# More filler products before the first batch's waits, and the second transposing read moved between the query and key moves

## The chip, the cores and the metric

The kernel runs on one core of a Trainium2 chip. The metric is the device time of one execution in microseconds (us), the median of several runs; lower is better.

## The reference

Strided sparse attention followed by a bilinear feed-forward layer. Shapes: q, k and v are 8 batches x 8 heads x 576 positions x 64; w_a and w_b are 512 x 1536, w_out is 1536 x 512; all inputs and the output are float32.

```python
scores = scale * np.matmul(q, k.transpose(0, 1, 3, 2))        # scale = 1/8
rel = pos[:, None] - pos[None, :]
mask_local   = (rel >= 0) & (rel < 32)
mask_strided = (rel >= 0) & (pos[None, :] % 32 == pos[:, None] % 32)
masks = [mask_local if h < 4 else mask_strided for h in range(8)]
attn = softmax(np.where(masks, scores, -1e9))
x = np.matmul(attn, v).transpose(0, 2, 1, 3).reshape(4608, 512)
out = ((x @ w_a) * (x @ w_b)) @ w_out
```

## The kernel before

**Two halves, woven together.** The feed-forward half works on nine tiles of 512 tokens (`t` = 0 to 8). A tile has 16 slots: 12 slots `ffn_ab`, one for each block `f` of 128 of the 1536 features (eight 128x128 by 128x512 products on TensorE, PE, in line 619; a copy on ScalarE, line 636; the product a*b on VectorE, lines 639 and 641), and 4 slots of output products (`ffn_y`, line 771, in tiles 0 and 1; `ffn_ys`, line 707, in tiles 2 to 8; `y_tail`, line 736, in the last). The attention half works on eight batches `b` of 576 tokens. Its steps are sent out between the slots, from tables written by hand: `STEPS` for batches 1 and 2, `LATER` for batches 3 to 7, by slot number. `take(i)` runs the attention steps due at slot `i`, and after it the functions registered with `do(i, ...)` for that slot run. All engines keep the written order (`manual_schedule`), and so does SP, the engine that issues most of the transfers inside the chip: an instruction that waits on SP holds back everything written behind it.

**Batch 0** comes before slot 0 and has an order of its own, the string `ORDER`. A name such as `Tk0p` is a part of a step: `Tk`/`Tq` transposes keys or queries on PE, `S` are scores (`p` the products, `x` the exponential on ScalarE, `m` the mask on VectorE), `V` is the product with the values (`p`) and its scaling (`r` a reciprocal, `n` the multiplication in line 489), `X` the transpose of the attention's output into `xT`, the feed-forward's input, and `F` the first feature blocks of tile 0. `*n` stands for `spin(n)`: n filler products of 128x128 by 128x224 constants on PE (line 154), whose results nobody reads.

**Batches 2 to 7** get their transposed keys and queries through `step_D`: VectorE transposes in blocks (line 326 for the first four heads, `z` = 0, in two parts; line 331 for the other four, `z` = 1, in three), and when the last part of the query is done, SP moves the pieces into place: for the query pair c=0 four transfers into `qz_buf` (line 345), then for the key pair c=1 two into `kT_buf` (line 341), then for the query pair c=1 four more. For batches 4 to 7, `step_D` of the last query part with `z` = 0 is registered for slot 16(b-2)+9.

**Batches 3 to 7, the first four heads' output.** It is written as rows to a scratch area in DRAM (`rows_out`, steps `O0` and `O1` in `LATER`, SP, line 504) and read back transposed into `xT` (`rows_in`, steps `I0` and `I1`, SP, line 509). `I1` of batch b is in `LATER` at 9, which is slot 16(b-1)+9: the same slot in which `step_D` of batch b+1 sends its moves, and ahead of them, since `take(i)` comes first.

```python
    LATER = {-1: "S0", 0: "S1", 1: "V0", 2: "S2", 3: "V1 O0", 4: "S3", 5: "V2", 6: "S4 I0", 7: "V3 O1", 8: "S5", 9: "V4 I1",
             10: "S6",
             11: "V5"}
```

The scores of the next batch begin one slot before the next tile (`-1: "S0"`, line 385) and read the pair c=0. The next tile's products read `xT` from its first slot on.

Of the kernel before, what the change touches and what calls it, by code (L numbers as in the profile page):

```python
# [14 lines left out]
FIRST_D = 2  # L15
# [15 lines left out]
def kernel(  # L31
# [11 lines left out]
    B, H, S, D = q.shape  # L43
# [134 lines left out]
    def blocks(nm, z):  # L178
        z = int(z)
        return sb.tile([128, 2, (S, RS * GP)[z]], BF16, tag=f"t{nm}{z}", name=f"t{nm}{z}", bufs=1)  # L180
# [138 lines left out]
    def step_D(b, z, nm, part):  # L319
        src = nats[b, nm, z == 1]  # L320
        if part == 0:
            tl[b, z, nm] = blocks(nm, z)
        t = tl[b, z, nm]
        if z == 0:
            i = slice(NY // 2 * part, NY // 2 * (part + 1))
            nc.vector.transpose(t.rearrange("p h (i y) -> p i h y", i=NY)[:, i],
                                src[:, i].rearrange("p i (h d) -> p i h d", h=2))
            last = part == 1
        else:

            nc.vector.transpose(
                t.rearrange("p h (r c) -> p r h c", r=RS)[:, :, :, YS * part:YS * part + 32],
                src[:, part].rearrange("p (r h d) -> p r h d", r=RS, h=2))
            last = part == 2
        if last:
            for nm, c in {"k": (("k", 0),), "q": (("q", 0), ("k", 1), ("q", 1))}[nm]:
                t = tl[b, z, nm]
                for e in range(2):
                    if nm == "k":
                        dst = kT_buf[b % 2][z][64 * e:64 * e + 64, c]  # L340
                        nc.sync.dma_start(out=dst[:, PAD:] if z == 0 else dst[:, :RS * GP], in_=t[64 * c:64 * c + 64, e])
                        continue
                    for j in range(2):
                        r0 = 64 * c + 32 * j
                        nc.sync.dma_start(out=qz_buf[b % 2][j][z][64 * e + 32 * j:64 * e + 32 * j + 32, c],
                                          in_=t[r0:r0 + 32, e])

    def rezero(b):

        for j in range(2):  # L350
            for t in qz_buf[b % 2][j]:
                nc.gpsimd.memset(t[32:64] if j == 0 else t[64:96], 0.0)
# [154 lines left out]
    def rows_in(b, c):  # L507

        nc.sync.dma_start(out=xT[:, c, S * (b % XR):S * (b % XR + 1)], in_=scratch.pop((b, c)), transpose=True)
# [51 lines left out]
    def step_X(b, c):  # L561
# [6 lines left out]
            "Xp": lambda c: X_p(0, c), "Xe": lambda c: X_e(0, c)}  # L568

    ORDER = """  # L570
        G0 C0 Tk0p *2 Tq0p Tk0e Tq0e *5 Tk1p S1p M G1 Tq1p S1x Tk1e *4 Tq1e S0p S1m *7 G2 C1 S0x S3p Tk2p Tq2p Tk2e S3x Tq2e *3
        S2p S2x V1p S0m *2 V1r S3m V0p V0r V1n V0n *2 S4p Tk3p Tk3e S2m Tq3p S4x Tq3e *2 S5p S5x X0p X0e *3 V2p V2r V3p V2n
        V3r V3n S6p V4p V4r V4n S6x X1p V5p V5r S7p X1e V5n V6p S7x F0A V6r V7p V6n X2p X2e Z F1A F0B V7r V7n F1B X3p F0b X3e
        F1b F0c F1c""".split()


# [2 lines left out]
                 12.6: "S1", 12.75: "L0 X2", 13: "s2 X3 V0 m2 L1 W3", 13.5: "V1 S3", 14: "V2 X0", 14.5: "V3 D1", 15: "X1"},  # L579
             2: {20: "S0", 20.5: "S1", 21.5: "V0", 22: "S2", 23: "V1", 23.5: "S3", 24.5: "V2", 25: "S4", 26: "V3", 26.5: "S5",  # L580
                 27.5: "V4", 28: "S6", 28.5: "V5", 29: "S7", 29.5: "V6", 30.5: "V7"}}
    LATER = {-1: "S0", 0: "S1", 1: "V0", 2: "S2", 3: "V1 O0", 4: "S3", 5: "V2", 6: "S4 I0", 7: "V3 O1", 8: "S5", 9: "V4 I1",
             10: "S6",
             11: "V5"}
    IN_Y = {2: "S7", 6: "V6", 11: "V7"}
    FN = {"Tk": step_Tk, "Tq": step_Tq, "S": step_S, "V": step_V, "X": step_X, "W": lambda b, n: fast_w(n, slice(0, 3)),
          "s": S_px, "m": S_m, "L": lead_vl, "O": rows_out, "I": rows_in, "Pk": lambda b, c: pair_up("k", c), "Pq": lambda b, c: pair_up("q", c),
          "Z": lambda b, n: zero_qz(0, nc.vector, ((1, 1),)), "D": lambda b, n: step_D(FIRST_D, 0, "k", n)}

    def run(b, slot):  # L590
# [4 lines left out]
    steps = {}  # L595
# [204 lines left out]
    with tc.manual_schedule(engines={ENG.PE, ENG.SP, ENG.Pool, ENG.DVE, ENG.Activation}):  # L800
# [76 lines left out]
        for b in range(1, B):  # L877
            for pos, names in (STEPS.get(b) or {16 * (b - 1) + x: n for x, n in LATER.items()}).items():
                steps.setdefault(pos, []).append((b, names.split()))
            if b not in STEPS:  # L880
                for n, names in IN_Y.items():
                    steps["y", b - 1, n] = [(b, names.split())]

        at = {}

# [12 lines left out]
        for b in range(FIRST_D, B):  # L898
            g0 = 16 * (b - 2)
            if b == FIRST_D:  # L900
                do(0, load_qk, b, False)
                do(1, load_qk, b, True)
                do(16, load_vl, b)
                for h in range(HL):
                    do(20 + h, load_vs, b, (h,))
            else:
                for h in range(HL):
                    do(g0 + h + (2 if b == FIRST_D + 1 else -2), load_qk, b, False, (h,))
                    do(g0 + h + (6 if b == FIRST_D + 1 else 2), load_qk, b, True, (h,))
                    do(g0 + h + 10, load_vs, b, (h,))  # L910
                do(g0 + (10 if b == FIRST_D + 1 else 7), load_vl, b)
            gs = {2: (14, 14, 15, 15, 16, 16, 17, 17, 18, 18), 3: (8, 9, 10, 11, 12, 13, 14, 15, 16, 17)}.get(b) or (
                3, 5, 7, 9, 12, 13, 14, 15, 16, 17)
            for (z, nm, part), g in zip(((0, "k", 0), (0, "k", 1), (0, "q", 0), (0, "q", 1), (1, "k", 0), (1, "k", 1),
                                         (1, "k", 2), (1, "q", 0), (1, "q", 1), (1, "q", 2)), gs):
                if (b, z, nm, part) != (FIRST_D, 0, "k", 1):
                    do(g0 + g, step_D, b, z, nm, part)
# [60 lines left out]
```

## Time and profile before

| | us |
|---|---|
| time, median of 3 runs (lowest, highest) | 328.95 (328.48, 330.82) |
| the profiled execution: its time | 331.59 |
| its span, first to last instruction | 329.6 |
| PE busy | 320.2 (97%) |
| VectorE (DVE) busy | 247.9 (75%) |
| ScalarE (ACT) busy | 183.5 (56%) |
| GpSimd (POOL) busy | 149.7 (45%) |
| mean granted TensorE clock | 0.987 of full |

The profile is of one execution. An engine's busy time is the sum over its instructions; those of PE overlap each other, so that a group of 12 products may show 1.47 us from its first start to its last end while the next group starts 1.31 us after it. The page cuts the span into 40 slices of 8.24 us and gives the busy share and the granted clock of PE for each, in tenths. In the timeline a row has the start in us, the duration in us, engine, line, operation, output and input, the count, and in brackets the idle time before it with what ended it. Rows of SPq are SP's queue issuing transfers: their duration is that of the issue, not of the landing.

### The profile page before, as it was taken

What the parts mean: (1) busy time and instruction counts of PE and PEld (TensorE: products, weight loads), DVE (VectorE), ACT (ScalarE), POOL (GpSimd) and SP (SyncE); (2) the same over time, 40 slices, a digit from 0 to 9 for tenths busy, and PEclk for the clock granted to TensorE, in tenths of its full rate; (3) what the DMA queues carried; (4) which work ended last, traced back from release to release, by engine and by line L of the source; (5) the groups of instructions that cost most, each with busy time, mean ns of one, the idle gap of its engine ahead of it and who ended that gap; (6) DMA issues with size and microseconds to landing.
All of it is one profiled execution on the core that took longest, in us unless ns stands there. A gap on an engine that the chain in (4) does not pass through costs nothing.

```text
span 329.6 us, 7240 instructions
## 1 busy us (share of the span) xinstructions
PE 320.2 (97%) x2597; PEld 204.6 (62%) x2624; DVE 247.9 (75%) x530; ACT 183.5 (56%) x305; POOL 149.7 (45%) x279
## 2 busy tenths in 40 slices
PE   7899999999999999999999999999999999999994
PEld 6664555455555578556999885559555954584474
DVE  7647687888868988898889888988977745726652
ACT  6744767358774476547654765467546643323341
POOL 8845836769857635762576337634101001100000
PEclk9959999999999999999999999999999999999998
DMA  9999999499999897999899999999145040004004
GB/s 156 153 204 194 204 183 165 136 161 144 119 234 118 152 109 76 113 206 137 93 126 182 173 100 100 173 185 113 45 107 139 16 127 0 3 0 129 0 0 127
DMA packets 110722, 40.41 MB, mean 123 GB/s; under 512 B 88672, under 2 KB 107744, under 8 KB 110688
## 3 DMA queue, kind: packets, MB, share of 16 engines
q0 software_dynamic: 85968, 19.48, 65.0%
q1 hardware_dynamic: 24576, 20.42, 24.6%
q8 instruction: 20, 0.33, 0.5%
q14 instruction: 14, 0.11, 0.1%
q10 hardware_dynamic: 144, 0.07, 0.1%
HBM read 39.51 MB, written 10.91 MB: 153 GB/s over the span
## 4 chain that ended last, share of the span: by engine, by line
PE 91%; DMA 3%; POOL 2%; DVE 1%; issue 1%; ACT 0%; POOLq 0%
PE mm L619 54%; PE mm L707 16%; PE mm L771 6%; PE st L385 4%; PE o L463 2%; PE o L522 2%; DMA vl<-in_v_dram 2%; PE mm L736 2%; PE ab L619 2%; POOL shared L196 1%; PE end L736 1%; DMA kT0l<-tk 1%; PE tp L547 1%; POOL vl L224 0%; PE tp L286 0%
## 5 line engine op out<-in xcount | busy, mean ns | idle before, releaser
L619 PE MATMUL mm<-xT,wb_sb 128*128 128x512 bf16 (+1 forms) x468 | 109.9, 357 | 0.5
L619 PE MATMUL mm<-xT,wa_sb 128*128 128x512 bf16 (+1 forms) x453 | 108.3, 356 | 0.7
L636 ACT COPY a_sb<-mm 128x512 f32<-128x512 f32 x106 | 62.0, 585 | 71.6 <-PE mm L619 70.7
L639 DVE TENSOR_TENSOR pf<-a_sb,mm 128x512 bf16<-128x512 f32 x84 | 57.3, 682 | 26.9 <-PE mm L619 22.4
L619 PEld LDWEIGHTS <-wb_sb 128*128 128x128 bf16 x480 | 46.7, 98 | 44.6 <-issue 1.1
L944 POOL CAST pace<-pf 1x1 f32<-1x1 bf16 x87 | 23.8, 274 | 110.8 <-DVE pf L639 94.2
L619 PEld LDWEIGHTS <-wa_sb 128*128 128x128 bf16 x480 | 43.8, 98 | 31.4 <-issue 0.2
L406 ACT ACTIVATE p<-st 72x576 bf16<-72x576 f32 (+1 forms) x56 | 36.4, 650 | 14.7 <-PE st L385 14.5
L538 DVE TENSOR_TENSOR xT<-o,xr 64x288 bf16<-64x288 f32 x48 | 21.4, 445 | 15.3 <-ACT xr L532 15.0
L707 PEld LDWEIGHTS <-ps 128*128 128x128 bf16 x288 | 28.0, 98 | 3.1
L707 PE MATMUL mm<-wf,ps 128*128 128x256 bf16 x216 | 25.5, 273 | 0.0
L684 ACT COPY y_sb<-mm 128x512 f32<-128x512 f32 (+1 forms) x28 | 15.5, 555 | 17.9 <-PE mm L707 14.5
L531 ACT ACTIVATE xr<-o 64x576 f32<-64x576 f32 x28 | 18.1, 647 | 12.2 <-PE o L522 12.0
L771 PE MATMUL mm<-wo_sb,pf 128*128 128x512 bf16 x93 | 23.1, 379 | 0.2
L242 POOL DMA_DIRECT2D vs<-in_v_dram x24 | 19.6, 818 | 5.1 <-PE mm L707 2.4
L707 PEld LDWEIGHTS <-pf 128*128 128x128 bf16 x216 | 20.3, 98 | 2.6 <-issue 0.2
L532 ACT ACTIVATE xr<-xr 64x576 f32<-64x576 f32 x28 | 19.1, 683 | 0.9
L707 PE MATMUL mm<-wo_sb,pf 128*128 128x256 bf16 x144 | 18.5, 273 | 0.1
L211 POOL DMA_DIRECT2D ql<-in_q_dram x24 | 16.1, 669 | 4.9 <-DMA wo_sb<-in_moe_w_out_dram 3.6
L211 POOL DMA_DIRECT2D kl<-in_k_dram x24 | 16.0, 668 | 4.9 <-issue 3.2
L641 DVE TENSOR_TENSOR pf<-a_sb,mm 128x512 bf16<-128x512 f32 x22 | 14.9, 676 | 4.3 <-ACT a_sb L636 2.7
L653 DVE TENSOR_TENSOR ps<-pf 128x512 bf16<-128x512 bf16 (+1 forms) x48 | 17.7, 380 | 0.4
(147 smaller groups left out, 453.3 us busy)
## 6 DMA issues: line engine op xcount, KB each, us to landing
out_dram<-y_sb SPq DMA_DIRECT2D x12, 512.0 KB, 4.9
out_dram<-y_sb SPq DMA_DIRECT2D x11, 256.0 KB, 3.0
vl<-in_v_dram POOLq DMA_DIRECT2D x6, 384.0 KB, 8.0
kl<-in_k_dram POOLq DMA_DIRECT2D x24, 72.0 KB, 3.2
ql<-in_q_dram POOLq DMA_DIRECT2D x24, 72.0 KB, 3.5
vs<-in_v_dram POOLq DMA_DIRECT2D x24, 72.0 KB, 4.2
wo_sb<-in_moe_w_out_dram POOLq DMA_DIRECT2D x4, 384.0 KB, 9.2
natk<-in_k_dram POOLq DMA_DIRECT2D x20, 72.0 KB, 3.6
```

The lines of the kernel that those rows point to most:

```text
L211: nc.gpsimd.dma_start(out=t[32 * h:32 * h + 32], in_=src[b, h].rearrange("(i y) d -> y i d", y=32))
L242: nc.gpsimd.dma_start(out=vs_buf[b % 2][:, h, :, 0:D], in_=v[b, HL + h].rearrange("(p r) d -> p r d", r=RS))
L406: nc.scalar.activation(p_flat(p)[:M, :2 * W].rearrange("p (i n) -> p i n", n=2 * n), st[:M].rearrange("p a (i n) -> p (a i) n", n=256)[:, ...
L531: nc.scalar.activation(r, sums, ACT.Ln)
L532: nc.scalar.activation(r, r, ACT.Exp, scale=-1.0)
L538: nc.vector.tensor_mul(dst.rearrange("d (p r) -> d p r", r=RS)[:, :, G * half:G * (half + 1)], o[:64, j, :W].rearrange("d (g p) -> d p g", ...
L619: nc.tensor.matmul(ps_[:, c0:c0 + n], lhsT=w[:, kk, 128 * f:128 * (f + 1)], rhs=xT[:, kk, x0:x0 + n], start=(kk == first and c0 == 0), sto ...
L636: nc.scalar.copy(a_sb, ab[0])
L639: nc.vector.tensor_mul(pf[:, f, :].rearrange("p (i a s) -> p a i s", i=2, s=16), halves(a_sb), halves(ab[1]))
L707: nc.tensor.matmul(bank[b][:, q], lhsT=lhs(g, q), rhs=rhs(g), start=k in "172" and q == 0 and g == 0, stop=g == FG - 1, skip_group_check=True)
L771: nc.tensor.matmul(ybank[j], lhsT=pf[:, f, 128 * j:128 * (j + 1)], rhs=wo_sb[:, f], start=(f == 0), stop=(f == FD - 1))
L944: nc.gpsimd.tensor_copy(pace, done)
```

## The change

There are two edits. In `ORDER`, three places get more fillers: after `Tk0p` 4 instead of 2, after `X0e` (before `V2p`) 5 instead of 3, and between `S6p` and `V4p` 4 where there were none. And `I1` is taken out of `LATER`; `step_D` now calls `rows_in(b - 1, 1)` itself, after the four moves of the query pair c=0 and before the moves of the key pair c=1, for b = 4 to 7, which are the reads of batches 3 to 6. For the last batch, which has no `step_D` after it, `I1` is appended to its old slot.

```diff
@@ step_D
                         nc.sync.dma_start(out=qz_buf[b % 2][j][z][64 * e + 32 * j:64 * e + 32 * j + 32, c],
                                           in_=t[r0:r0 + 32, e])
+                if (nm, c, z) == ("q", 0, 0) and b - 1 > FIRST_D:
+                    rows_in(b - 1, 1)
@@ ORDER
-        G0 C0 Tk0p *2 Tq0p Tk0e Tq0e *5 Tk1p S1p M G1 Tq1p S1x Tk1e *4 Tq1e S0p S1m *7 G2 C1 S0x S3p Tk2p Tq2p Tk2e S3x Tq2e *3
-        S2p S2x V1p S0m *2 V1r S3m V0p V0r V1n V0n *2 S4p Tk3p Tk3e S2m Tq3p S4x Tq3e *2 S5p S5x X0p X0e *3 V2p V2r V3p V2n
-        V3r V3n S6p V4p V4r V4n S6x X1p V5p V5r S7p X1e V5n V6p S7x F0A V6r V7p V6n X2p X2e Z F1A F0B V7r V7n F1B X3p F0b X3e
+        G0 C0 Tk0p *4 Tq0p Tk0e Tq0e *5 Tk1p S1p M G1 Tq1p S1x Tk1e *4 Tq1e S0p S1m *7 G2 C1 S0x S3p Tk2p Tq2p Tk2e S3x Tq2e *3
+        S2p S2x V1p S0m *2 V1r S3m V0p V0r V1n V0n *2 S4p Tk3p Tk3e S2m Tq3p S4x Tq3e *2 S5p S5x X0p X0e *5 V2p V2r V3p V2n
+        V3r V3n S6p *4 V4p V4r V4n S6x X1p V5p V5r S7p X1e V5n V6p S7x F0A V6r V7p V6n X2p X2e Z F1A F0B V7r V7n F1B X3p F0b X3e
@@ LATER
-    LATER = {-1: "S0", ..., 7: "V3 O1", 8: "S5", 9: "V4 I1",
+    LATER = {-1: "S0", ..., 7: "V3 O1", 8: "S5", 9: "V4",
@@ after the steps are entered
+        steps[16 * (B - 2) + 9][-1][1].append("I1")
```

## The prediction

> **What bounds the kernel now.** I read the page first, by engine and by slice, then the chain of waits, then what TensorE (PE) waited for, then the timelines of PE and of SP's queue around the places that the diff touches.
>
> ```profile
> PE 320.2 (97%) x2597; PEld 204.6 (62%) x2624; DVE 247.9 (75%) x530; ACT 183.5 (56%) x305; POOL 149.7 (45%) x279
> ...
> PE   7899999999999999999999999999999999999994
> ...
> PEclk9959999999999999999999999999999999999998
> ...
> PE 91%; DMA 3%; POOL 2%; DVE 1%; issue 1%; ACT 0%; POOLq 0%
> ```
>
> PE is busy 97% of the span and is 91% of the chain that ended last. So a change can give back only what PE loses to waits, or to a low clock. The clock row shows one hole: the third slice stands at half. Cut finer, in windows of half the hole's length (6.8 us, from 17.2 to 24.0):
>
> ```profile
> 13.81:17.22 3.41, 2.44 (x61) 1.98 (x59) 1.88 (x6) 1.76 (x4) 2.49 (x4) 1.00 1.34 179
> 17.22:20.63 3.41, 3.17 (x62) 2.62 (x59) 2.35 (x6) 1.17 (x2) 1.36 (x3) 0.50 1.32 204
> 20.63:24.04 3.41, 3.41 (x20) 1.60 (x18) 0.72 (x2) 1.75 (x3) 1.35 (x2) 0.50 1.26 205
> ```
>
> The column after the five busy times is the granted clock: 1.00, then 0.50 from 17.2 to 24.0 us. In the window before the fall PE was busy 2.44 of 3.41 us (72%). The PE timeline says where it idled:
>
> ```profile
> 5.30 0.36 PE L154 MATMUL misc<-const-bfloat16-1.0 128*128 128x224 bf16 x2
> 6.12 0.43 PE L286 MATMUL tp<-ident,shared 96*128 96x96 bf16 x6 [0.46 <-ACT shared L837]
> ...
> 13.77 0.46 PE L154 MATMUL misc<-const-bfloat16-1.0 128*128 128x224 bf16 x3
> 14.86 0.52 PE L463 MATMUL o<-vl,p 128*128 128x65 bf16 x12 [0.63 <-DMA vl<-in_v_dram]
> ...
> 16.07 0.20 PE L463 MATMUL o<-tk,p 72*128 72x64 bf16 x1 [0.33 <-DVE xr L489]
> ```
>
> Three idle gaps: 0.46, 0.63 and 0.33 us. The diff puts its fillers into exactly these. After 24 us only one wait of a PE matmul is left in the whole execution, in the stage of tile 4; SP's queue beside it:
>
> ```profile
> 183.48 1.27 SPq L509 DMA_TRANSPOSE xT<-xd  x1
> 184.85 0.53 SPq L504 DMA_DIRECT2D xd<-xl  x1
> 190.58 1.15 SPq L509 DMA_TRANSPOSE xT<-xd  x1
> 191.82 2.46 SPq L345 DMA_DIRECT2D qz0l<-tq  x4
> 194.38 1.18 SPq L341 DMA_DIRECT2D kT0l<-tk  x2
> 195.60 2.49 SPq L345 DMA_DIRECT2D qz0l<-tq  x4
> ```
>
> ```profile
> 195.92 1.47 PE L707 MATMUL mm<-wo_sb,ps 128*128 128x256 bf16 x12
> 197.87 0.41 PE L385 MATMUL st<-qz0l,kT0l 128*128 128x192 bf16 x3 [0.47 <-DMA kT0l<-tk]
> ```
>
> The transposing read (L509, "I1") stands at the head of SP until the copy issued at 184.85 has landed (5.1 us of waiting), and the first query moves stand behind it. They are issued from 191.82 to 194.28 and land up to 5.0 us later in this window, while the scores want them at 195.92 + 1.31 = 197.23 (the same group of 12 takes 1.31 at 128.07, 161.74 and 230.22, where nothing waits). They start at 197.87: 0.64 us lost.
>
> **Part 1: eight more fillers.** From the rows of filler groups, 2 take 0.36 us and 7 take 0.86: each further one costs 0.10, the first 0.26 with its drain. Two more before the query transposes end at 5.66 + 0.20 = 5.86, before the cast that ends the gap at 6.12: no cost, ScalarE's cast is the cover. Two more before V2 end at 14.23 + 0.20 = 14.43, before the values land at 14.81: no cost, the DMA is the cover. Four new ones before V4 must fit between 15.74 and 16.07: they take 0.40 if they follow the scores without a gap, 0.57 with their drain; the cover is VectorE's row scaling (L489, 0.55 us from 15.46). Cost between 0.07 and 0.24 us; I take 0.1. Behind V4 on PE's queue stand X1, V5 and S7, so this shift would pass on. If the covers were gone, all eight would cost 8 x 0.10 = 0.8.
>
> What the fillers may bring is the clock. At the half clock the 512-wide products of L619 run at 1.91 us for 4 (21.55) against 1.03 (26.48). I price the hole by walking the stage at full speed: S7 and V6 end 0.35 us sooner, the first product group starts at 18.65 instead of 19.15, V7, X2 and the next six products take 2.4 instead of 4.1, X3 and the last eight products 2.1 instead of 2.4. The first product of feature block 2 then starts near 23.2 instead of 25.62: 2.4 us. The low bound counts the dense products alone (20.7 to 24.0 at half speed): 1.7. The other bound is nothing: the clock falls all the same. For the fillers: the window before the fall would be busy 2.44 + 0.2 + 0.33 = 2.97 of 3.41 us, 87% instead of 72%. Against: the second window was busy 3.17 of 3.41 (93%) and still did not bring the clock back; it is full of 64- and 1-column products (L463, L465), and the fillers do not touch those. I take it that in this very execution the hole is averted or shortened, with a chance of a little over a half.
>
> The Trainium skill, in "TensorE: Matmul & The Clock Gate", section "What's actually happening", says the clock is set from activity in free-running windows of 3413 ns that do not start with the kernel. The hole of 17.2 to 24.0 us is two such windows, so row and rule agree on the length; the rule adds that the fall depends on where a window happens to lie, so some executions would have no hole. Its section "HAM oscillation" asks for idle gaps above about 3.4 us before the clock falls; by that, fillers in gaps of 0.63 us would be needless and the sum would hold no clock term; the trace contradicts it, as its longest gap here is 0.63 us.
>
> **Part 2: I1 moved past the first four query moves.** Nothing is added or removed: for batches 3 to 6 the same transposing read (1.14 us on SP) goes behind four moves (2.46 us together) of the next batch. What these wait for is VectorE's second query transpose (L326), done at 118.78, 152.45, 186.32 and 220.93; I1 started at 116.42, 156.13, 190.58 and 224.91. In three of the four the query is ready 3.7 to 4.3 us before I1 leaves the head of the queue. So there the four moves go out in the wait for the copy, 4.9 to 5.4 us sooner, I1 stays where it was, and the key and query moves of the second pair come 2.5 us sooner (their SP time of 2.46 us now lies in the wait). In tile 4 the query lands by 186.4 + 2.5 + 5.0 = 193.9, 3.3 us ahead of the scores: the 0.64 us go. In the other tiles PE doesn't wait, so nothing is gained (the scores start at 163.05 and 231.53, with moves issued until 159.82 and 228.62 and landing up to 3.8 and 3.6 later: they are within 1 us of a wait, which the change also insures). Batch 3 is the odd one: the query is ready only at 118.78, so I1 goes from 116.42 to about 121.3, and the later moves 1.2 us back. Its rows are first read by the products of tile 3 at 129.63, and 121.3 + 3.4 (its landing there) = 124.7: 4.9 us to spare. The cost is nothing while that cover stands; if it went, each us beyond would be a us of PE.
>
> **The sum**, against the profiled execution, 331.59 us (span 329.6 and 2.0 around it): - 0.64 (part 2) + 0.1 (fillers) - 2.4 (hole) = 328.65; with the hole left, 331.05. The median of the runs shown is 328.95, 2.64 below the profiled execution, and their spread, 328.48 to 330.82, is 2.34: about the price of one hole. I read this as a hole that two of the three timed runs did not have, or had shorter. The median then has little of it to give back: 328.95 - 0.64 + 0.1 - 0.3 (a share of a shorter hole) = 328.1. About 1% (3.3 us) is what a measurement of this kernel can tell from no change.
>
> **The rivals.**
> 1. The median run does have the hole, and the fillers close it: 328.95 - 0.54 - 2.4 = 326.0. For it: the clock row, and the fillers stand exactly in the idle gaps before the fall. Against: the 2.64 us between profiled and timed executions would then need another reason. Chance 0.22; a third of it, with other tiles' near waits also removed, passes 1%.
> 2. Nothing moves: the hole stays, and in timed runs the query lands in time anyway, as it did in three of four tiles: 328.95 + 0.1 = 329.05. For it: those three tiles, and the 93% window that stayed at half. Chance 0.15.
> 3. Slower: the fillers hold the clock through the first weak window, and it falls one window later, over the dense products. Place: 20.6 to 27.4 us instead of 17.2 to 24.0. Price: 6.8 us at half speed on products that PE could otherwise run without a break, 3.4 us, where the old hole cost 2.4 and a run without one nothing: 328.1 + 3.4 = 331.5, or 329.1 against a holed median. It decides if the window with V4 to V7 (64-column products, 16.07 to 20.3) is weak by itself at full speed. Against: the dense products from 20.7 on should refill a window at once. Chance 0.10.
> 4. That the move does not do what it says: SP holds the queue in order, so if VectorE's transpose came as late as in batch 3 in all tiles, I1 and all behind it would slip by 1 to 5 us; with 4.9 us to spare, 328.95 again. It is counted with rival 2.
>
> **How the numbers follow.** The forecast, 328.1, has a chance of 0.53, its own range 327.3 to 328.8. The range 325.8 to 329.9 takes in rival 1 at its price, rival 2 and the holed end of rival 3, and leaves out most of rival 3's 331.5 and the deep end of rival 1. Faster by over 1% (below 325.7): 0.15, from rival 1 and from a hole that costs more than the walk says. Slower by over 1% (above 332.2): 0.06, the far end of rival 3. Within 1%: 0.79.
>
> **What would show it.** Right: the clock row without the 5 in the third slice, the first product of block 2 near 23.2 us, V4 not later than 16.3; on SP in tile 4 the four query moves from about 186.4, I1 at 190.6, and no wait of the scores (L385) near 197. Wrong: a 5 in the fourth slice (rival 3), the same 5 in the third (rival 2), or a PE wait for xT at the start of a tile. A median below 325.8 would show that I read the timed runs' share of the hole wrongly.

## The result, and the profile after

| | before | after |
|---|---|---|
| median of 20 runs each (lowest, highest), us | 329.04 (327.72, 334.28) | 327.48 (327.13, 328.48) |
| ratio, 95% interval | | 0.9946 [0.9926, 0.9966] |
| the profiled execution: time, span, us | 331.59, 329.6 | 327.27, 325.6 |

The change is about half a percent faster: below the 1% that was set as the bound, but clear of no change. The forecast was 328.1. Ratios here and below leave out runs more than 1.5% above the fastest of the same kernel; medians, ranges and the counts of runs with a low clock take in every run.

The page of after, engine by engine and slice by slice, against the lines shown of before:

```profile
PE 319.7 (98%) x2632; PEld 204.6 (63%) x2632; DVE 247.9 (76%) x530; ACT 183.6 (56%) x305; POOL 150.3 (46%) x279
...
PE   8999999999999999999999999999999999999994
...
PEclk9999999999999999999999999999999999999999
```

The 5 in the third slice is gone. The same three windows (the number after the five busy times and their counts is the granted clock):

```profile
13.81:17.22 3.41, 3.41 (x85) 3.04 (x81) 2.38 (x7) 2.36 (x4) 2.66 (x5) 1.00 1.35 185
17.22:20.63 3.41, 3.41 (x67) 2.25 (x60) 2.42 (x6) 2.23 (x4) 1.28 (x2) 1.00 1.32 204
20.63:24.04 3.41, 3.41 (x17) 1.55 (x16) 1.57 (x3) 2.43 (x5) 1.35 (x2) 1.00 1.25 205
```

PE is busy all the time and the clock stays at 1.00. The PE timeline at the two later filler places has no idle bracket any more:

```profile
13.86 0.66 PE L154 MATMUL misc<-const-bfloat16-1.0 128*128 128x224 bf16 x5
14.36 0.53 PE L465 MATMUL o<-vl,p 128*128 128x65 bf16 x12
...
15.17 0.56 PE L154 MATMUL misc<-const-bfloat16-1.0 128*128 128x224 bf16 x4
15.57 0.20 PE L465 MATMUL o<-tk,p 72*128 72x64 bf16 x1
```

V4 starts 1.21 us after V2, as before (16.07 - 14.86): the four new fillers cost nothing. Feature block 2 (the products `mm`) starts at 22.21 instead of 25.62, 3.41 us sooner. The first product group and the first product of block 2, before and then after:

```profile
19.15 0.63 PE L619 MATMUL ab<-xT,wa_sb 128*128 128x512 bf16 x1 [0.24 <-ACT p L409]
...
25.62 1.03 PE L619 MATMUL mm<-xT,wa_sb 128*128 128x512 bf16 x3
```

```profile
17.74 0.59 PE L621 MATMUL ab<-xT,wa_sb 128*128 128x512 bf16 x2
...
22.21 1.03 PE L621 MATMUL mm<-xT,wa_sb 128*128 128x512 bf16 x4
```

And SP's queue in tile 4, with the first scores behind it:

```profile
180.23 1.30 SPq L511 DMA_TRANSPOSE xT<-xd  x1
181.62 1.99 SPq L506 DMA_DIRECT2D xd<-xl  x1
183.71 2.46 SPq L345 DMA_DIRECT2D qz0l<-tq  x4
187.22 1.16 SPq L511 DMA_TRANSPOSE xT<-xd  x1
188.47 1.18 SPq L341 DMA_DIRECT2D kT0l<-tk  x2
```

```profile
192.53 1.47 PE L709 MATMUL mm<-wo_sb,ps 128*128 128x256 bf16 x12
193.84 0.41 PE L387 MATMUL st<-qz0l,kT0l 128*128 128x192 bf16 x3
```

The four query moves go out while the copy lands; the scores follow the products at the usual 1.31 us, without a wait. (In before the bracket of this wait names a key move, but the weight load just ahead of the scores waited 0.6 us for a query move.) The span is 4.0 us shorter: 3.41 before block 2, and some 0.6 in tile 4.

But both profiles are single executions, and that of before was an unlucky one. The experiments separate what these executions show from what the median gained.

### The profile page after: what moved, and what is told of

Same layout as the page of the kernel before. It is cut to its first block, busy times and chain, and to the rows that moved or that the text cites. A ratio compares the mean times of both kernels' runs of the same rounds, so it can differ in the third digit from the quotient of the medians.

```text
span 325.6 us, 7280 instructions
## 1 busy us (share of the span) xinstructions
PE 319.7 (98%) x2632; PEld 204.6 (63%) x2632; DVE 247.9 (76%) x530; ACT 183.6 (56%) x305; POOL 150.3 (46%) x279
## 4 chain that ended last, share of the span: by engine, by line
PE 94%; DMA 2%; DVE 1%; ACT 1%; issue 1%; POOL 0%; POOLq 0%
PE mm L621 54%; PE mm L709 17%; PE mm L773 6%; PE st L387 4%; PE o L465 2%; PE o L524 2%; DMA shared<-in_q_dram 2%; PE mm L738 2%; PE end L738 1%; PE ab L621 1%; PE misc L154 1%; PE tp L549 1%; PE tp L295 1%; PE st L400 0%; PE tp L286 0%
## 5 line engine op out<-in xcount | busy, mean ns | idle before, releaser
L621 PE MATMUL mm<-xT,wa_sb 128*128 128x512 bf16 (+1 forms) x472 | 110.3, 357 | 0.0
L947 POOL CAST pace<-pf 1x1 f32<-1x1 bf16 x87 | 23.7, 273 | 109.6 <-DVE pf L641 93.1
```

The source lines that it names most:

```text
L621: nc.tensor.matmul(ps_[:, c0:c0 + n], lhsT=w[:, kk, 128 * f:128 * (f + 1)], rhs=xT[:, kk, x0:x0 + n], start=(kk == first and c0 == 0), sto ...
L947: nc.gpsimd.tensor_copy(pace, done)
```

## The experiments

All comparisons are with before, run on the same chip in the same rounds.

**Before again, and each half alone.** Three kernels and after itself, run side by side.

> The kernel before again, so that each of its runs is seen with its granted clock. If the hole of the clock makes the spread of this kernel, runs with a mean clock near 0.987 should take about 331 us and runs near 1.0 about 328.5, in a line of some 0.25 us for each 0.001 of clock; if transfers make the spread (the values of the first batch, or the query moves of tile 4), time and clock should not go together. Ratio 1.000.

Measured: 0.9993 [0.9965, 1.0021], median 329.75 (328.08 to 330.52). Time and clock do not go together: the runs near 330.5 have clocks of 0.994 to 0.998, and a run at a full 1.0 took 329.99. So the hole is not what spreads these twelve runs. The profile of this repeat has no hole (block 2 at 22.08) and yet loses time elsewhere, in tile 6:

```profile
221.84 1.13 SPq L509 DMA_TRANSPOSE xT<-xd  x1
223.06 2.48 SPq L345 DMA_DIRECT2D qz1l<-tq  x4
```

```profile
226.27 1.47 PE L707 MATMUL mm<-wo_sb,ps 128*128 128x256 bf16 x12
228.84 0.42 PE L385 MATMUL st<-qz1l,kT1l 128*128 128x192 bf16 x3 [1.10 <-DMA qz1l<-tq]
```

The scores were due at 226.27 + 1.31 = 227.58: 1.26 us lost, to the same queue order that cost 0.64 in tile 4 of the first profile.

The fillers alone:

```diff
 (before, with the new ORDER; LATER and step_D as before)
```

> The fillers alone, the transposing read left in its old place. By the theory that the fillers keep the clock up: the clock of every run near 1.0, no time near 331, the median 0.5 to 1.5 us under before (ratio 0.995 to 0.998), and the scores of batch 6 still waiting up to 0.6 us for the query moves. By the rival that the moved read brings the gain: ratio 0.999 to 1.001 with runs at 0.987 as before.

Measured: 1.0002 [0.9971, 1.0032], median 329.45 against 330.01 of before and 329.75 of its repeat; the clock between 0.995 and 1.0. No gain that this measurement can tell. The profile waits 0.82 us for the query moves in tile 6: the scores start at 228.38, 0.98 us after they were due (226.09 + 1.31 = 227.40).

The moved read alone:

```diff
 (after, with the ORDER of before)
```

> The moved read alone, fillers as before. By the theory that the two edits give separate gains: the median 0.3 to 0.6 us under before (ratio 0.998 to 0.999), runs with a low clock as often as before and the spread as wide. By the rival that the read brings the whole gain: ratio 0.9945 and a narrow spread. In the profile no wait of the scores near 197 us, and the four query moves of batch 6 issued some 5 us sooner.

Measured: 0.996 [0.9939, 0.9982], median 328.28: 1.7 us under before by the medians, 1.3 by the ratio, two to three times the upper end of what was expected, and no wait of the scores in the profile. Its lowest clock is 0.996, without any of the new fillers.

> Both edits again, on the same chip as the two halves. If the gains add up, its gain is the sum of those of the two halves within 0.4 us; ratio 0.9946 within 0.002, the clock between 0.996 and 1.0 in every run.

Measured: 0.9941 [0.9919, 0.9962], median 327.45 (327.11 to 328.27). The halves' ratios, 0.996 and 1.0002, make 0.9962, 0.7 us short of it. That is more than the 0.4 expected, but the interval of either half is wide enough for it.

**Is it the place ahead of the read, or the copy's landing?** Two kernels change the order in other ways. In the first the four moves go behind the six others:

```diff
-            for nm, c in {..., "q": (("q", 0), ("k", 1), ("q", 1))}[nm]:
+            for nm, c in {..., "q": (("k", 1), ("q", 1), ("q", 0)) if b > FIRST_D + 1 and z == 0 else ...}[nm]:
```

> Before, with the four moves of the query pair c=0 put behind the moves of the second pair for batches 4 to 7 (the reading transfer stays ahead of all ten). They go out 1.17 + 2.50 = 3.7 us later. By the theory that the first scores wait for just these moves and that a us of their lateness is a us of TensorE: in batch 4 nothing (it had 5 us to spare), in batches 5, 6 and 7 some 3.3 to 4.5 us each, 10 to 13 us in all, ratio 1.030 to 1.040, with waits of the scores named in three tiles. By the rival that the scores wait for all ten moves whatever their order: ratio within 0.002 of 1.

Measured: 1.0189 [1.0114, 1.0263] from two of the four runs, 335.28 (the profiled one) and 338.81; the other two took 341.56 and 342.13 us, 3.6 and 3.7% over before. The scores wait in three tiles, as expected, and the steps from one batch's first scores to the next grow by 1.47, 1.77 and 2.26 us (the first: 126.39 to 161.53 is 35.14 instead of 33.67). So the rival that the order does not matter falls. In the profiled execution the price per tile is about half of what was guessed: the last of the four moves landed 1.9 to 2.3 us after its issue, where the last of the four in before took 3.0 to 4.1. But this was the fastest of the four runs, and the two slowest lie where they were expected, so the usual price stays open. The wait costs more than itself:

```profile
233.41 0.41 PE L385 MATMUL st<-qz1l,kT1l 128*128 128x192 bf16 x3 [2.09 <-DMA qz1l<-tq]
...
236.75 1.59 PE L619 MATMUL mm<-xT,wa_sb 128*128 128x512 bf16 x4
238.17 1.03 PE L619 MATMUL mm<-xT,wb_sb 128*128 128x512 bf16 x4
```

After this wait the clock falls (0.62 from 234 to 236, 0.53 from 236 to 238), and four products take 1.59 us where they take 1.03 at the full clock. After the waits of 1.31 and 1.62 us in the two tiles ahead it stayed at 1.00.

In the second the copy (`O1`) is taken off SP, so that it lands sooner, and the read stays in its old place:

```diff
-        nc.sync.dma_start(out=scratch[b, c]...)
+        (nc.scalar if c == 1 else nc.sync).dma_start(out=scratch[b, c]...)
```

> Before, with the second copy to the scratch area issued by ScalarE's queue instead of SP's, so that it no longer stands behind SP's backlog and the first transposing read; the order of SP is else that of before. By the theory that the copy's landing is what holds the query moves: the reading transfer and the query moves of batches 5 to 7 leave 2 to 4 us sooner, the waits of the scores go and the ratio is near that of the moved read alone, 0.995 to 0.998. By the rival that it is the order of the transfers itself (the read and the moves side by side) that costs: 0.999 to 1.001. ScalarE pays some 0.6 us of issue for each copy, hidden as long as it is busy 56%.

Measured: 0.9973 [0.9944, 1.0002], median 329.36 against 329.82. In its profile the moves of batch 6 leave at 185.71, with the read ahead of them, and no scores wait in any tile: the copy's landing is what held the moves. The time leans the same way, but its interval just reaches 1, so the profile carries this finding and not the time.

**Must the read stand between query and key?** After, with the read behind all ten moves:

```diff
-                if (nm, c, z) == ("q", 0, 0) and b - 1 > FIRST_D:
+                if (nm, c, z) == ("q", 1, 0) and b - 1 > FIRST_D:
```

> After, with the transposing read put behind all ten moves instead of behind the first four. By the theory that only the first four have to be out before the read: the same gain, ratio 0.993 to 0.996, the read 3.7 us later at most and its rows still in time (4.9 - 3.7 = 1.2 us to spare in batch 3). By the rival that part of the gain comes from where the read stands between query and key: slower than after by 1 us or more, with a wait of the first products of a tile for xT.

Measured: 0.9925 [0.9892, 0.9957], median 328.17 against 329.82 of its own rounds. The gain is there too, and no product waits for xT. What matters most is that the first four moves are out before the read. The median is 0.6 us above that of after in the other comparisons (327.54), which no run beside it can settle.

**What do the fillers do?** After without the fillers at the three places, and after without any of the first batch's fillers:

```diff
-  Tk0p *4 Tq0p ... X0e *5 V2p ... S6p *4 V4p
+  Tk0p Tq0p ... X0e V2p ... S6p V4p
```

> After, without any filler at the three places (before it: 4, 5 and 4; in the kernel before: 2, 3 and none). By the theory that fillers in these gaps keep the clock up: most runs with a mean clock of 0.98 to 0.99 and some 2.4 us more, a median of 329 to 330 (ratio 0.998 to 1.002). By the rival that the fillers do nothing there: the time of after or of the moved read alone, ratio 0.994 to 0.996, the clock between 0.996 and 1.0.

Measured: 0.9958 [0.9922, 0.9995], median 328.07. Ten of 12 runs have a clock of 0.996 or more and 327.04 to 328.77 us; the other two have 0.989 and 0.984, and 330.46 and 331.82 us. Neither theory as written: not most runs, but not none.

> Both edits, but with all fillers of the first batch taken out (45 in ten places; the 23 at the very start stay). By the theory that the fillers hold the clock up in the stage of the first batch: the clock falls there in most runs, a mean clock of 0.97 to 0.99, and the time rises by 2 to 5 us, a median of 329.5 to 332. By the rival that the clock is decided elsewhere: 327.3 to 328.5, clock 0.996 to 1.0.

(The fillers taken out are 38 in ten places, not 45.) Measured: 1.0068 [1.004, 1.0095], median 331.56, the clock 0.971 to 0.979 in all eight runs. Against 327.54, the median of the 41 runs of after, this is 4.0 us. The hole is wider and stands in two slices:

```profile
PEclk9659999999999999999999999999999999999999
```

So fillers do hold the clock up in this stage. But most of that work was done by those that were there before: with them alone the clock is low in some runs, not in all (counted below).

> The moved read alone a second time, beside both edits on the same chip, to see whether the new fillers bring anything once the read is moved. By the theory that they only insure against an occasional fall of the clock: the medians of this and of both edits within 0.4 us of each other, with a low clock (below 0.993) in none to two runs of 12 here. By the rival that they bring a steady gain: this one 0.8 us slower, as in the first comparison, in its fastest runs too.

Measured: 0.9962 [0.9939, 0.9984], median 328.11; two of the 13 runs have a low clock, 0.987 (332.05 us) and 0.989, the profiled one, 330.89 us. Its profile shows a hole without the new fillers, as the first profile did:

```profile
14.06 0.46 PE L154 MATMUL misc<-const-bfloat16-1.0 128*128 128x224 bf16 x3
15.32 0.52 PE L465 MATMUL o<-vl,p 128*128 128x65 bf16 x12 [0.80 <-DMA vl<-in_v_dram]
...
16.53 0.20 PE L465 MATMUL o<-tk,p 72*128 72x64 bf16 x1 [0.33 <-DVE xr L491]
...
26.18 1.03 PE L621 MATMUL mm<-xT,wa_sb 128*128 128x512 bf16 x4
```

The values landed late, PE idled 0.80 us, the clock fell at 18.2 and came back at 25.0, and block 2 started 10.86 us after V2. In the first profile of the same kernel, without a hole, it is 7.86:

```profile
14.26 0.53 PE L465 MATMUL o<-vl,p 128*128 128x65 bf16 x12
...
22.12 1.03 PE L621 MATMUL mm<-xT,wa_sb 128*128 128x512 bf16 x4
```

That prices a hole at 3.0 us.

> Both edits, beside the moved read alone: ratio 0.992 to 0.996, median 327.3 to 327.8, no run with a clock below 0.993.

Measured: 0.9951 [0.993, 0.9971], median 327.65, lowest clock 0.997. Its profile has a wait for the values too (0.32 us, at 14.52) and no hole.

**A version that might beat both.** After, with the second load of values issued sooner:

```diff
-        load_qk(0, True, (2, 3))
         load_vl(0, (12, 24))
+        load_qk(0, True, (2, 3))
```

> Both edits, and the load of the values for the heads 2 and 3 of the first batch issued ahead of the two loads of keys and queries for the strided heads 2 and 3 (1.4 us sooner on GpSimd's queue). It aims at the wait of V2, up to 0.6 us. By the theory that this wait is on the path: block 2 of tile 0 starts 0.2 to 0.6 us sooner and the median is 326.9 to 327.4. By the rival that the two displaced loads are then late for their transposes at 12.4 us: 327.5 to 328.5.

Measured: 0.999 [0.9961, 1.002], median 328.61: a miss. The rival was right, a little beyond its 328.5. The displaced loads are late: the strided transposes (L295) wait 1.0 us for `shared`, and block 2 starts at 23.61. No kernel run here has a median below those of after (327.45 to 327.65).

## Why the prediction was right or wrong

**The clear part.** The forecast of a small gain, within 1%, held, and its two mechanisms are both real. The shares were wrong: it gave the moved read 0.64 us and the clock 0.3 of the median's gain. The gain that was forecast, 0.85 us, is about half of the 1.56 between the medians; that 327.48 still lies in the forecast's own range, 327.3 to 328.8, owes something to luck.

**Part 2, the moved read: the mechanism right, the term too small.** Alone it brings 1.7 us by the medians of the first comparison and 1.4 by those of the second (329.49 to 328.11), 1.3 by either ratio. The step that failed is "in the other tiles PE doesn't wait, so nothing is gained": it took one execution's waits for those of all. The prediction itself noted that tiles 3 and 6 were within 1 us of a wait; in the repeat of before tile 6 lost 1.26 us and tile 4 nothing worth naming, with the fillers alone tile 6 again. A wait with less than a us to spare, in three tiles, behind transfers whose landing varies by about as much (the last of the four moves took 3.0 to 4.1 us in one profile), should have been priced as an expected loss in each. The three profiles with SP's order of before lost 0.64, 1.26 and 0.98 us so; what the moved read gains beyond that, no profile shows. The change doesn't touch a like wait of batch 2, which has no read ahead of its moves: 0.35 us at 65.85 in the repeat of before, 0.51 at 66.26 without the three filler groups. The other numbers of this step came out: batch 3's read went from 116.42 to 117.99 in a stage that now runs some 3.4 us sooner, 121.4 on the old scale against 121.3 predicted; the reads of the other batches stayed where they were; rows for the next tile were never late. Rival 4 (the queue slips behind VectorE) did not happen.

**Part 1, the cost of the fillers: right.** 0.1 us was taken; none is seen (V2 to V4 1.21 us before and after).

**Part 1, the hole: the mechanism right, the price too small.** Block 2 was predicted near 23.2 and came at 22.21. Half a us of the difference is not the clock: the values landed sooner and V2 started at 14.36. From V2 on, the stage took 7.85 us instead of 10.76, 2.9 less, against the walk's 2.4; the pair of profiles of the moved read alone gives 3.0. The walk's first step was the short one: from V2 to the first product group it is 3.38 us instead of 4.29, 0.9 less where the walk took 0.5 off. The next two steps came out at 2.43 and 2.04 us, against 2.4 and 2.1.

**The median and the spread: wrong reading, near number.** "The spread is about the price of one hole" failed. A hole of 6.8 us at half clock takes 0.010 off an execution's mean clock, and the profiles without one show 0.996 to 1.000, so a mean below 0.993 can serve as its mark; a fall half as long would not show. Of the runs of before and its repeat whose clock is on record, 11 of 100 have it; their median is 331.89 us. The other 89 spread from 326.85 to 334.43 us without it, around 329.53. What the median gained is thus mostly the moved read's, the waits of the scores as far as profiles show it, and rival 1, which made the hole the median's, is out. Rival 3 was not seen: no profile with the new fillers shows a fall before the last 3 us of the span.

**The fillers' share.** Runs below 0.993: none of 41 of after, none of 12 of the fillers alone, none of 8 with the read last; without the new fillers 11 of 100 of before, two of 25 of the moved read alone, two of 12 without the three groups, one of 12 with the copy off SP. (Two kernels have new waits of their own: two of 12, 0.992 and 0.978, where the values are loaded first, with the fillers in place; three of 4 where the query moves go last.) That is what insurance looks like, and a hole of 3 us in one run of nine moves a mean and hardly a median. The medians still differ: 328.25 for the moved read alone (25 runs), 327.54 for both (41 runs), 0.71 us, and 328.16 if the two runs with a low clock are left out. The fillers alone can't be it, as the kernel with the read last has them too and a median of 328.17. In the one profile of the moved read alone without a hole, block 2 starts at 22.12 (21.84, 22.21 and 22.37 with both edits), and from there to the last addition on VectorE it is 299.6 us (299.2 to 299.6); some 0.7 us lies behind that addition, 4.79 us to the end of the span where the three profiles with both edits have 4.0 to 4.2. Whether the median's 0.7 us lies there too, one profile can't tell. This stays open.

## What to carry to other kernels

A wait on an in-order queue charges everything written behind it: write first what is ready and urgent, then what must wait, and check only that the waiting one still meets its own reader. Price a near miss (less than a us to spare behind a transfer) as an expected loss, even where the one profile at hand shows none. And before the spread of runs is put down to one cause, look whether that cause's mark, here the granted clock, goes with the time: here it marked some of the slowest runs and not the rest of the spread.

## What the runs showed of the hardware

The clock fell after less idleness than expected. In the profiles with a hole the longest idle gaps of PE just before it were 0.63 and 0.33 us, or 0.80 and 0.33, and without any filler of the first batch 0.63 and 0.36; with one wait of 2.09 us in the middle of dense products it fell too. The gaps alone do not decide it: without the three groups PE idled 0.54 and 0.34 us at the same two places, in a profile whose clock stayed at 1.00 there. In "HAM oscillation" of "TensorE: Matmul & The Clock Gate" the Trainium skill speaks of gaps above about 3.4 us; these runs show falls well below that. The lengths of the falls, 6.8 us (17.2 to 24.0 and 18.2 to 25.0), 13.7 (10.0 to 23.7, without any filler) and 3.4 (234.5 to 237.9, behind the wait of 2.09), do fit two, four and one of the windows that the page's "What's actually happening" gives, 3413 ns each. Its free-running windows would also explain why the same kernel has a hole in some executions only, but no run here shows where a window begins.

The end of an execution also varies by a us where no computing instruction does: from the last addition on VectorE to the end of the span it was 4.0 to 4.3 us in most profiles and 4.79 and 5.04 in two. It is the last write of the output that lands later: 3.3 and 3.4 us after its issue in these two, 2.5 in the profile of after.
